# FFN tiles three to eight: the first four column blocks computed by token halves, and one query transpose six slots sooner

## The chip, the core and the metric

The kernel runs on one core of a Trainium2 chip. The core has a matrix engine (TensorE, PE in the profile), three engines that compute on vectors (VectorE or DVE, ScalarE or ACT, GpSimd or POOL), and a sync engine (SyncE or SP) that here only issues DMAs. TensorE reads its operands from the on-chip memory SBUF and writes to the accumulators in PSUM, of which this kernel uses eight banks of 128 x 512 fp32. Every matmul instruction is preceded by a weight load (PEld), which the profile shows on a row of its own. The metric is the device time of one launch in microseconds (us), the median of several runs.

## The reference

Two stages follow each other. The first is linear attention over 8 batches, 8 heads, 576 positions and a head size of 64; the second is a multiplicative feed-forward network (FFN) on its 4608 tokens.

```
r = max(x, 0);  phi(x) = [r * cos(theta), r * sin(theta)]      # 64 -> 128 features, for q and k
kv  = sum over positions of phi(k) v^T         z = sum of phi(k)
x   = (phi(q) kv) / (phi(q) z + 1e-6)          # 4608 tokens x 512
a, b = x @ w1, x @ w2                          # 512 -> 1024 each
out = ((a * b) @ w3) @ w_out                   # 1024 -> 1024 -> 512
```

## The kernel before

**Tiles.** The tokens of all batches are laid in a row and cut into nine FFN tiles of 512 tokens, which the code numbers 0 to 8. A tile's input `xT` has features on the partitions and tokens along the free dimension. Because a batch has 576 tokens, a tile's tokens come from two batches, in pieces of 128 (or 64) that finish at different times.

**How a tile's input is made.** For each piece c of batch b the plan names these steps: `q b c` makes the query features `qp` (DVE the cosine half, ACT the sine half, L494 to L502; a number at the end leaves only that many heads to ACT and the rest to DVE), `qd b c` transposes them by a DMA of SP's queue into `qpT` (L521), `n b c` multiplies them with `kvs` on TensorE (L580), `d b c` divides by the denominator on DVE (L591 to L593) into `xblk`, and `xd b c` transposes that by another DMA of SP's queue into its columns of `xT` (L613). `k`, `v` and `kv` prepare the state `kvs` of a batch; `kv` is 40 matmuls of 65 columns (L548).

**How a tile is computed.** `ffn_groups(t)` is a generator; each `f t` of the plan runs it to its next `yield`, which is a step. For each of eight column blocks of 128 (`jc`) there are two steps. In the first, four matmuls of 512 tokens with `w1b` (L667) give `aT`, and ACT copies it to SBUF as `asb` (L708). In the second, four matmuls with `w2b` give `bT`, and DVE multiplies both into `abT` (L714). The PSUM tiles come from a pool of four banks, `ffn_tile()`, taken in rotation: a step's bank is the one of four PSUM tiles earlier, and it is free when ACT or DVE has read it. Tiles 0 and 1 compute their first four blocks differently, in halves and quarters of the tokens (`on_half`), two blocks to a bank.

For the second stage, `w3 @ w_out` has been multiplied once into `w34b`. Tiles 2 to 7 (`SEVEN`) use seven products of half-sized blocks in place of eight (`seven_products`, L794), for which DVE forms sums of quarters of `abT` (`sums`, L774) and adds the products up (L802). In the pairs of tiles the last products of one tile and the first steps of the next take turns, as the plan has it:

```
f 3; k 5 3 4; k 5 2; v 5 1 V; lg 6 k 0; q 5 3
f 4
f 3; lt 7 k 0; d 4 3
f 4; qd 5 0
f 4; n 4 4
```

**What sets the order.** The order is written by hand in `PLAN`, read from top to bottom; each engine and each queue executes its own instructions in that order, and waits by semaphores. In a line, `f t` comes first and then what its neighbours do. `lt` and `sx` let POOL wait for the DMA transpose that was named last before it in the plan, and then issue a load or a store; `lg` and `sg` do the same with the latest `asb`.

In the code, tile 4 is the one whose first step `f 4` stands in the lines above (L139); `qd 6 1` stands at L189, between `xd 6 4` (L184) and `xd 6 2` (L190), and `n 6 1`, which reads its result, at L193. The features `q 6 1 4` stand at L179.

Of the kernel before, what the change touches and what calls it, by code (L numbers as in the profile page):

```python
# [11 lines left out]
BF16 = mybir.dt.bfloat16  # L12
# [4 lines left out]
P = 128  # L17
# [162 lines left out]
f 5  # L180
f 5; xd 6 0
f 5
f 5; n 6 4
f 5; d 6 4; xd 6 4  # L184
f 5
f 5; n 6 2
f 5
f 6; v 7 3 V; n 6 3
f 6; qd 6 1; d 6 2; q 7 2; sg  # L189
f 6; xd 6 2; gx 0; q 7 4 2  # L190
f 6; d 6 3; sg; q 7 0
f 6; qd 7 4; k 7 4; xd 6 3
# [65 lines left out]
f 8  # L258
f 8"""
SEVEN = (2, 3, 4, 5, 6, 7)  # L260
ON_POOL = (8,)
NKP, NVA, NQP, NRQ, NRV, NT3 = 1, 2, 1, 2, 2, 3

# [50 lines left out]
def kernel(  # L314
# [11 lines left out]
    nc = tc.nc  # L326
# [10 lines left out]
    fsb = ctx.enter_context(tc.tile_pool(name="fsb", bufs=3))  # L337
# [21 lines left out]
    w1b = const.tile([P, 4, DFF], BF16, name="w1b")  # L359
    w2b = const.tile([P, 4, DFF], BF16, name="w2b")  # L360
# [59 lines left out]
    def load_q04():  # L420
# [5 lines left out]
                      in_=q[0, :, 0:512, :].rearrange("h (p j) d -> p h (j d)", j=4))  # L426
# [197 lines left out]
    newest = [None]  # L624
# [29 lines left out]
    def ffn_tile():  # L654

        return ffn_pool[0].tile([P, 512], FP32, name="ffnps")

    def ffn_groups(t):
        x = xT[t]
        abT = None  # L660

        def new_abT():
            return fsb.tile([P, 8, 512], BF16, name="abT", bufs=1)

        def products(out, w, jc, tok):
            for kc in range(4):
                nc.tensor.matmul(out, lhsT=w[:, kc, ts(jc, 128)], rhs=x[:, kc, tok],  # L667
                                 start=(kc == 0), stop=(kc == 3))

        def on_half(half):  # L670

            for pair in range(2):
                a, b = ffn_tile(), ffn_tile()
                if pair == 0:
                    for quarter in range(2):
                        for i in range(2):
                            for ps, w in ((a, w1b), (b, w2b)):
                                products(ps[:, ds(256 * i + 128 * quarter, 128)], w, i,
                                         ds(256 * half + 128 * quarter, 128))
                            if half == 0 and quarter == 0 and i == 0:  # L680
                                yield
                        if quarter == 0:
                            yield
                else:
                    for ps, w in ((a, w1b), (b, w2b)):
                        for i in range(2):
                            products(ps[:, ts(i, 256)], w, 2 + i, ts(half, 256))
                        if half == 0 and w is w1b:
                            yield
                asb = fsb.tile([P, 512], BF16, name="asb")  # L690
                nc.scalar.copy(out=asb[:], in_=a[:, :])
                newest[0] = asb
                nc.vector.tensor_mul(out=abT[:, ts(pair, 2), ts(half, 256)],
                                     in0=asb[:].rearrange("p (i n) -> p i n", i=2),
                                     in1=b[:, :].rearrange("p (i n) -> p i n", i=2))
                yield

        seven = t in SEVEN
        s = [fsb.tile([P, 4, 256], BF16, name=f"s{i}", bufs=1) for i in range(3)] if seven else None
        if t <= 1:  # L700
            abT = new_abT()
            yield from on_half(0)
            yield from on_half(1)
        for jc in range(4 if t <= 1 else 0, 8):
            aT = ffn_tile()
            products(aT[:, :], w1b, jc, slice(0, 512))
            asb = fsb.tile([P, 512], BF16, name="asb")
            nc.scalar.copy(out=asb[:], in_=aT[:, :])  # L708
            newest[0] = asb
            yield  # L710
            bT = ffn_tile()
            products(bT[:, :], w2b, jc, slice(0, 512))
            abT = abT or new_abT()
            nc.vector.tensor_mul(out=abT[:, jc, :], in0=asb[:], in1=bT[:, :])  # L714
            if seven and jc == 3:
                sums(abT, s, 0, 4, 3)
            if seven and jc == 5:
                sums(abT, s, 0, 2, 2, 1)
            if seven and jc == 7:
                sums(abT, s, 2, 2, 2, 1)  # L720
                sums(abT, s, 0, 4, 4)
            yield
# [31 lines left out]
    def A_of(abT, r, c, i0=0, n=4):  # L754

        return abT[:, ds(4 * c + i0, n), ts(r, 256)]
# [10 lines left out]
    def sums(abT, s, i0, n, *which):  # L767

        s3, s2, s4 = (x[:, ds(i0, n)] for x in s)
        a11, a12, a21, a22 = (A_of(abT, r, c, i0, n) for r in range(2) for c in range(2))  # L770
        for i in which:
            out, a, b, op = {3: (s3, a11, a21, ALU.subtract), 1: (a21, a21, a22, ALU.add),
                             2: (s2, a22, s3, ALU.subtract), 4: (s4, a12, s2, ALU.subtract)}[i]
            nc.vector.tensor_tensor(out=out, in0=a, in1=b, op=op)  # L774

    def seven_products(t, abT, s):
# [4 lines left out]
        last = t == NT - 1  # L781
        side = nc.gpsimd if t in ON_POOL else nc.vector
        u3, u4 = (x[:].rearrange("p c m -> p (c m)").bitcast(FP32) for x in (s2, s3))
# [140 lines left out]
    def store_behind_transposes():  # L924

        gate(transposed[0])
        store_next()

    ffn = [ffn_groups(t) for t in range(NT)]
    do = {  # L930
        "f": lambda t: next(ffn[t]), "w": w34_mm, "w3": load_w3, "wo": load_wout, "w12": w12,
# [45 lines left out]
```

## Time and profile before

| | before |
|---|---|
| median of 3 runs | 246.83 us (246.6 to 247.05) |
| the profiled execution's own time | 246.72 us |
| its span in the profile | 244.9 us |
| TensorE busy | 235.6 us, 2035 matmuls |
| VectorE busy | 191.4 us, 455 instructions |
| ScalarE busy | 111.7 us |
| GpSimd busy | 79.8 us |
| granted TensorE clock | 1.00 |

The span is the part of the time that the profile covers; 1.8 us lie around it. A row of the timeline has the start in us, the length in us, the engine, the line of the kernel, the operation, what it writes and reads, the shape, and in brackets how long the engine stood idle before it and what ended that. The ends of matmuls are modelled, so the pace of TensorE is read from one group's start to the next one's. In a row of the windows, the numbers are the length of the stretch and then, for each engine, the busy time and the number of instructions.

### The profile page before, as it was taken

Reading aid. Unit: us, or ns where it says so; the run is one execution under the profiler, and the core shown is the slowest. Engines: PE = TensorE matmul, PEld = TensorE weight load, DVE = VectorE, ACT = ScalarE, POOL = GpSimd, SP = SyncE. Lnnn points to the kernel's source line nnn. Section 1 sums busy time; section 2 is a strip of 40 time slices with the busy share of each in tenths; the row PEclk is TensorE's granted clock in tenths of the full one; section 3 lists DMA queues with packets and bytes.
Section 4 is the critical chain, followed back from the end, with each engine's and each line's share of the span. In section 5 each row is a group of like instructions: output and inputs, shape, how many; then the busy total and the mean of one; then the engine's idle time right before and its main releaser. Section 6 shows DMA issues by size and latency. Waiting matters only on the chain.

```text
span 244.9 us, 5395 instructions
## 1 busy us (share of the span) xinstructions
PE 235.6 (96%) x2035; PEld 144.5 (59%) x2035; DVE 191.4 (78%) x455; ACT 111.7 (46%) x198; POOL 79.8 (33%) x152
## 2 busy tenths in 40 slices
PE   8899999999999999999996999999989999999994
PEld 2589544566964544765583548555835675484443
DVE  6876577968888758999889798999999688776320
ACT  2833333677655733835472435737164412322321
POOL 8754887634503124107206103401020031084000
PEclk9999999999999999999999999999999999999999
DMA  7999999999999899969997998699297627499963
GB/s 198 191 196 199 197 179 193 199 198 174 154 166 162 131 153 169 197 115 148 141 176 99 192 174 110 72 175 155 33 232 136 119 44 181 88 272 315 262 185 128
DMA packets 84938, 40.47 MB, mean 165 GB/s; under 512 B 48048, under 2 KB 82096, under 8 KB 84912
## 3 DMA queue, kind: packets, MB, share of 16 engines
q0 software_dynamic: 37616, 23.60, 66.4%
q1 hardware_dynamic: 47296, 16.52, 39.3%
q8 instruction: 16, 0.26, 0.4%
q14 instruction: 10, 0.08, 0.1%
HBM read 38.80 MB, written 9.44 MB: 197 GB/s over the span
## 4 chain that ended last, share of the span: by engine, by line
PE 81%; DVE 10%; DMA 6%; issue 1%; DVEq 0%; ACT 0%; ACTq 0%
PE ffnps L667 47%; PE ffnps L794 7%; PE ffnps L729 7%; PE unread L456 4%; PE ffnps L473 4%; DMA xT<-xblk 3%; PE pnum L548 3%; PE pnum L580 3%; DMA qpT<-qp 2%; PE ffnmore L794 1%; DVE xblk L593 1%; DVE kp L494 1%; PE pst L566 1%; DVE qp L494 1%; PE pst L620 1%
## 5 line engine op out<-in xcount | busy, mean ns | idle before, releaser
L667 PE MATMUL ffnps<-xT,w1b 128*128 128x512 bf16 (+2 forms) x352 | 76.0, 340 | 2.4 <-DMA xT<-xblk 2.2
L667 PE MATMUL ffnps<-xT,w2b 128*128 128x512 bf16 (+2 forms) x352 | 76.0, 340 | 0.0
L708 ACT CAST asb<-ffnps 128x512 bf16<-128x512 f32 x64 | 37.5, 585 | 79.0 <-PE ffnps L667 60.5
L714 DVE TENSOR_TENSOR abT<-asb,ffnps 128x512 bf16<-128x512 bf16 x64 | 43.5, 682 | 20.8 <-PE ffnps L667 20.6
L667 PEld LDWEIGHTS <-w1b 128*128 128x128 bf16 x352 | 31.6, 98 | 30.0 <-issue 3.0
L667 PEld LDWEIGHTS <-w2b 128*128 128x128 bf16 x352 | 31.4, 98 | 26.8
L593 DVE TENSOR_TENSOR xblk<-pnum,den 128x512 bf16<-128x512 f32 (+1 forms) x39 | 26.9, 691 | 1.3
L498 ACT ACTIVATE kp<-kf,sinv 128x512 bf16<-128x512 bf16 (+4 forms) x33 | 20.4, 654 | 2.6 <-DMA kf<-in_k_dram 2.6
L418 POOL COPY seen<-xT 128x1 bf16<-128x1 bf16 x6 | 1.1, 189 | 61.1 <-DMA xT<-xblk 61.1
L729 PE MATMUL ffnps<-w34b,abT 128*128 128x512 bf16 x88 | 20.8, 379 | 0.0
L794 PEld LDWEIGHTS <-abT 128*128 128x128 bf16 x192 | 18.5, 98 | 3.2
L580 PEld LDWEIGHTS <-qpT 128*128 128x128 bf16 x320 | 15.1, 98 | 7.3 <-DMA qpT<-qp 1.6
L498 ACT ACTIVATE qp<-qs,sinv 128x512 bf16<-128x512 bf16 (+6 forms) x30 | 18.3, 626 | 1.7 <-DMA qpT<-qp 0.7
L580 PE MATMUL pnum<-kvs,qpT 128*128 128x65 bf16 x312 | 16.1, 194 | 1.1 <-DMA qpT<-qp 1.1
L794 PEld LDWEIGHTS <-s 128*128 128x128 bf16 x144 | 14.0, 98 | 2.0
L494 DVE TENSOR_SCALAR kp<-kf,cosv 128x512 bf16<-128x512 bf16 (+1 forms) x40 | 14.6, 385 | 0.0
L473 PE MATMUL ffnps<-early,w3T 128*128 128x512 bf16 x64 | 14.3, 379 | 0.0
L418 POOL COPY seen<-asb 128x1 bf16<-128x1 bf16 x13 | 2.8, 218 | 34.5 <-ACT asb L708 34.5
L729 PEld LDWEIGHTS <-abT 128*128 128x128 bf16 x88 | 8.1, 98 | 8.5
L794 PE MATMUL ffnps<-w34b,abT 128*128 128x256 bf16 x96 | 12.4, 273 | 0.0
L494 DVE TENSOR_SCALAR qp<-qs,cosv 128x512 bf16<-128x512 bf16 (+1 forms) x35 | 11.9, 349 | 0.5 <-issue 0.5
L513 POOL COPY va<-vs 128x512 bf16<-128x512 bf16 (+1 forms) x13 | 8.4, 654 | 10.9 <-DMA vs<-in_v_dram 10.3
(127 smaller groups left out, 322.0 us busy)
## 6 DMA issues: line engine op xcount, KB each, us to landing
out_dram<-osb SPq DMA_DIRECT2D x9, 256.0 KB, 3.5
kf<-in_k_dram POOLq DMA_DIRECT2D x7, 320.0 KB, 6.9
early<-in_moe_w_dram POOLq DMA_DIRECT2D x16, 128.0 KB, 5.1
qs<-in_q_dram POOLq DMA_DIRECT2D x6, 320.0 KB, 8.0
vs<-in_v_dram POOLq DMA_DIRECT2D x6, 320.0 KB, 8.1
kf<-in_k_dram POOLq DMA_DIRECT2D x7, 256.0 KB, 7.2
qs<-in_q_dram POOLq DMA_DIRECT2D x6, 256.0 KB, 9.5
vs<-in_v_dram POOLq DMA_DIRECT2D x6, 256.0 KB, 9.3
```

The lines of the kernel that those rows point to most:

```text
L456: nc.tensor.matmul(unread[:, :], lhsT=zeros[:, 0:128], rhs=zeros[:], start=True, stop=True)
L473: nc.tensor.matmul(acc[:, :], lhsT=w3T[:, lc, :], rhs=woutb[:, lc, :], start=(lc == 0), stop=(lc == 7))
L494: nc.vector.tensor_scalar(out=dst[:R, c, :, 0:D], in0=rows[:R], scalar1=0.0, scalar2=cosv[:R, at:at + 1], op0=ALU.max, op1=ALU.mult)
L498: nc.scalar.activation(out=dst[:R, c, 0:n, D:F], in_=rows[:R, 0:n], func=ACTF.Relu, scale=sinv[:R, at:at + 1], bias=0.0)
L513: (copy or nc.gpsimd.tensor_copy)(out=att_of(b)["va"][:R, c, :, 0:D], in_=raw[b, "v"][:R, :, c, :])
L580: nc.tensor.matmul(nt[:, h // 4, ds((h % 4) * 65, 65)], lhsT=qpT[:, h, ds(at, 128)], rhs=kvs[:, h, :], start=True, stop=True)
L593: nc.vector.tensor_tensor(out=xblk[rows, g0:g0 + ng], in0=n4[:, :, :, 0:D], in1=den[rows, 0:ng].unsqueeze(3).to_broadcast([R, ng, 4, D]), ...
L667: nc.tensor.matmul(out, lhsT=w[:, kc, ts(jc, 128)], rhs=x[:, kc, tok], start=(kc == 0), stop=(kc == 3))
L708: nc.scalar.copy(out=asb[:], in_=aT[:, :])
L714: nc.vector.tensor_mul(out=abT[:, jc, :], in0=asb[:], in1=bT[:, :])
L729: nc.tensor.matmul(ops[:, :], lhsT=abT[:, jc, ts(ms, 128)], rhs=w34b[:, jc, :], start=(jc == 0), stop=(jc == 7))
L794: nc.tensor.matmul(into[:, ts(ms, 256)], lhsT=a[:, kc, ts(ms, 128)], rhs=b[:, kc, :], start=(ms == 0 and kc == 0), stop=(ms == 1 and kc == 3))
```

## The change

Two things change. In tiles 2 to 7 the first four column blocks are no longer computed one block at a time over 512 tokens, but two blocks at a time over 256 tokens: first both pairs of blocks for one half of the tokens, then both for the other half. Tile 3 takes the upper half first, the other tiles the lower half. A step still fills one PSUM bank, with eight matmuls of 256 columns in place of four of 512; the number of steps, of ACT copies and of DVE multiplications stays, and the DVE operation for the differences of quarters (`sums(..., 3)`) follows the eighth step as before. The matmuls with the tile's first half wait only for the transposes that write that half.

Secondly the DMA transpose `qd 6 1` moves up by six lines of the plan, ahead of `xd 6 4` in SP's queue. In the list of instructions, SP's queue has just these two exchanged; GpSimd's is the same as before.

```diff
 f 5
-f 5; n 6 4
+f 5; n 6 4; qd 6 1
 f 5; d 6 4; xd 6 4
...
 f 6; v 7 3 V; n 6 3
-f 6; qd 6 1; d 6 2; q 7 2; sg
+f 6; d 6 2; q 7 2; sg
...
 SEVEN = (2, 3, 4, 5, 6, 7)
+BY_HALF = {t: (1, 0) if t == 3 else (0, 1) for t in range(2, 8)}
...
-        for jc in range(4 if t <= 1 else 0, 8):
+        if t in BY_HALF:
+            for half, pair in [(h, p) for h in BY_HALF[t] for p in range(2)]:
+                aT = ffn_tile()
+                for i in range(2):
+                    products(aT[:, ts(i, 256)], w1b, 2 * pair + i, ts(half, 256))
+                asb = fsb.tile([P, 512], BF16, name="asb")
+                nc.scalar.copy(out=asb[:], in_=aT[:, :])
+                newest[0] = asb
+                yield
+                bT = ffn_tile()
+                for i in range(2):
+                    products(bT[:, ts(i, 256)], w2b, 2 * pair + i, ts(half, 256))
+                abT = abT or new_abT()
+                nc.vector.tensor_mul(out=abT[:, ts(pair, 2), ts(half, 256)],
+                                     in0=asb[:].rearrange("p (i n) -> p i n", i=2),
+                                     in1=bT[:, :].rearrange("p (i n) -> p i n", i=2))
+                if seven and half == BY_HALF[t][1] and pair == 1:
+                    sums(abT, s, 0, 4, 3)
+                yield
+        for jc in range(4 if t <= 1 or t in BY_HALF else 0, 8):
             aT = ffn_tile()
             products(aT[:, :], w1b, jc, slice(0, 512))
```

## The prediction

> **What bounds the kernel.** I read the page's busy shares first, then TensorE's waits, then its timeline for the place of each, then the same stretches for VectorE and SP.
>
> ```profile
> PE 235.6 (96%) x2035; PEld 144.5 (59%) x2035; DVE 191.4 (78%) x455; ACT 111.7 (46%) x198; POOL 79.8 (33%) x152
> ```
>
> ```profile
> PE ffnps L667 <- DMA xT<-xblk: 2.2, 1, 2.2
> ...
> PE pnum L580 <- DMA qpT<-qp: 1.1, 1, 1.1
> ```
>
> TensorE is busy nearly throughout, and two of its three longest waits are for DMA transposes. They are these:
>
> ```profile
> 127.54 1.04 PE L794 MATMUL ffnps<-early,abT 128*128 128x256 bf16 x8
> 130.72 1.02 PE L667 MATMUL ffnps<-xT,w1b 128*128 128x512 bf16 x4 [2.15 <-DMA xT<-xblk]
> ...
> 136.17 1.03 PE L667 MATMUL ffnps<-xT,w2b 128*128 128x512 bf16 x4
> ```
>
> ```profile
> 181.03 1.03 PE L667 MATMUL ffnps<-xT,w2b 128*128 128x512 bf16 x4
> 183.18 0.43 PE L580 MATMUL pnum<-kvs,qpT 128*128 128x65 bf16 x8 [1.11 <-DMA qpT<-qp]
> ...
> 187.76 1.03 PE L667 MATMUL ffnps<-xT,w2b 128*128 128x512 bf16 x4
> ```
>
> A group takes 0.87 us from start to start (pace below), so the first gap is 130.72 - 127.54 - 0.87 = 2.31 us, before tile 4's first step; the second is 183.18 - 181.03 - 0.86 = 1.29 us, before `n 6 1`. Both have their late transposes in SP's queue:
>
> ```profile
> 113.87 1.33 SPq L613 DMA_TRANSPOSE xT<-xblk  x1
> 119.44 1.19 SPq L613 DMA_TRANSPOSE xT<-xblk  x1
> 122.22 2.27 SPq L613 DMA_TRANSPOSE xT<-xblk  x1
> ...
> 173.00 1.19 SPq L613 DMA_TRANSPOSE xT<-xblk  x1
> 176.34 1.17 SPq L613 DMA_TRANSPOSE xT<-xblk  x1
> 177.60 2.17 SPq L521 DMA_TRANSPOSE qpT<-qp  x1
> ```
>
> Counted off against the plan, these are `xd 3 3`, `xd 4 0`, `xd 4 1`, then `xd 6 0`, `xd 6 4`, `qd 6 1`. Tile 4's lower half is `xd 3 2` and `xd 3 3`, issued by 113.87; what it waits for is `xd 4 1` in its upper half, issued at 122.22 and landed at 130.7.
>
> But VectorE is the second bound. Busy time by stretch (length, then PE, PEld, DVE, ACT, POOL, then granted clock, DMA and GB/s):
>
> ```profile
> 153.00:159.40 6.40, 6.40 (x42) 3.34 (x40) 6.33 (x19) 4.48 (x9) 2.75 (x5) 1.00 0.71 75
> ...
> 172.00:178.00 6.00, 6.00 (x68) 4.88 (x67) 5.59 (x14) 0.80 (x2) 0.00 (x0) 1.00 0.18 33
> 178.00:183.20 5.20, 4.08 (x20) 1.69 (x19) 5.06 (x15) 3.47 (x7) 1.49 (x4) 1.00 0.96 230
> 183.20:190.00 6.80, 6.80 (x73) 3.97 (x74) 6.66 (x18) 2.68 (x5) 0.00 (x0) 1.00 0.74 152
> 190.00:196.00 6.00, 6.00 (x48) 3.87 (x45) 3.58 (x9) 2.58 (x5) 0.00 (x0) 1.00 0.60 115
> ```
>
> In 153 to 159.4 VectorE works 6.33 of 6.40 us, in 178 to 190 11.72 of 12.0 us. It does not become free when TensorE's wait goes, so a gain has to pass through it. From 190 on it has room (3.58 of 6.0).
>
> **Part 1, halves: what goes at tile 4.** The lower half landed long before 128.4, so step one can start at 128.41. The upper half is first read in step five, over four us later, when `xd 4 1` has landed (130.7). The 2.31 us wait goes. What is late next is VectorE, through the four PSUM banks.
>
> ```profile
> 130.59 0.69 DVE L802 TENSOR_TENSOR osb<-ffnps,s 128x512 f32<-128x512 f32 x1
> 132.66 0.69 DVE L802 TENSOR_TENSOR osb<-ffnps,s 128x512 f32<-128x512 f32 x1 [0.19 <-PE ffnps L794]
> 134.91 1.36 DVE L714 TENSOR_TENSOR abT<-asb,ffnps 128x512 bf16<-128x512 bf16 x2
> ...
> 137.30 0.69 DVE L714 TENSOR_TENSOR abT<-asb,ffnps 128x512 bf16<-128x512 bf16 x1 [0.77 <-PE ffnps L667]
> ```
>
> From 128 to 132.66 VectorE has other work and idles only 0.19 us, so it can run 0.19 us sooner, no more. I walk through the banks. Step a0 starts at 128.41, tile 3's last product at 129.28, b0 at 130.15. a1 needs the bank that the row at 130.59 reads, free at 131.28. `n 4 4` and b1 follow until 133.3, a2 until 134.1. b2 needs the bank of b0, which VectorE reads in the first of the two at 134.91, now 134.72, free at 135.40. So b2 starts at 135.40 where it started at 136.17: 0.77 us of the 2.31 come through, and 1.54 turn into a wait for a bank.
>
> Further on the gain meets a load.
>
> ```profile
> 147.40 0.19 POOL L418 COPY seen<-xT 128x1 bf16<-128x1 bf16 x1 [11.73 <-DMA xT<-xblk]
> 147.85 0.68 POOL L375 DMA_DIRECT2D kf<-in_k_dram  x1 [0.27 <-issue]
> ...
> 153.26 0.40 ACT L498 ACTIVATE kp<-kf,sinv 128x128 bf16<-128x128 bf16 x1 [2.13 <-DMA kf<-in_k_dram]
> 153.26 0.35 DVE L494 TENSOR_SCALAR kp<-kf,cosv 128x512 bf16<-128x512 bf16 x1
> ```
>
> ACT waits 2.13 us for keys that are loaded behind an SP transpose, and VectorE takes the same keys at the same 153.26, with no idle time before it only because it was busy until then. If the load moves with the rest, 0.77 us survive. If SP's chain, whose members hang on rows that move by 0.19 us only, sets the load, VectorE waits and about 0.2 us survive. I take the middle, 0.45 us; nothing in the trace decides it.
>
> **Part 1, halves: what it costs.** 32 matmuls of 512 become 64 of 256 in each of six tiles: 192 matmuls and 192 weight loads more. The pace of both forms is in the trace, the short one in tile 0:
>
> ```profile
> 24.09 1.04 PE L667 MATMUL ffnps<-xT,w1b 128*128 128x256 bf16 x8
> 24.96 1.04 PE L667 MATMUL ffnps<-xT,w2b 128*128 128x256 bf16 x8
> 25.84 1.03 PE L667 MATMUL ffnps<-xT,w1b 128*128 128x512 bf16 x4
> ...
> 220.68 1.03 PE L667 MATMUL ffnps<-xT,w1b 128*128 128x512 bf16 x4
> 221.54 1.03 PE L667 MATMUL ffnps<-xT,w2b 128*128 128x512 bf16 x4
> ...
> 233.63 1.03 PE L667 MATMUL ffnps<-xT,w2b 128*128 128x512 bf16 x4
> ```
>
> Eight of 256 take 0.87 to 0.88 us; four of 512 take (233.63 - 220.68) / 15 = 0.863. The added weight loads are hidden in that pace. A step so costs 0.007 to 0.017 us more, 0.01 say; 48 steps, 0.48 us. In tiles 4, 5 and 6 (24 steps) VectorE or a bank is waited for anyway, so half of it shows: 0.24 us, between 0 and 0.8. VectorE's multiplication with a split output is priced in tiles 0 and 1, 686 ns (L693) against 682 ns (L714):
>
> ```profile
> L714 DVE TENSOR_TENSOR abT<-asb,ffnps 128x512 bf16<-128x512 bf16 x64 | 43.5, 682 | 20.8 <-PE ffnps L667 20.6
> ...
> L693 DVE TENSOR_TENSOR abT<-asb,ffnps 128x512 bf16<-128x512 bf16 x8 | 5.5, 686 | 3.4 <-ACT asb L691 2.1 <-PE ffnps L667 1.3
> ```
>
> For 24 of them this is 0.1 us at most, taken as nothing. At the start of tiles 2, 3, 5, 6 and 7 the waits list has no wait for `xT`, so the halves remove nothing there; they only keep a wait from arising if these tiles start sooner. In tile 3 the order of the halves only changes which transposes come first.
>
> A rule of the Trainium skill speaks against this part. The page "TensorE: Matmul & The Clock Gate", section "Back-to-back issue gap", says that a stream of weight loads and matmuls runs at some 81 ns for 128 columns and 131 ns for 512. On a straight line a 256-column matmul would take an estimated 98 ns, two of them 65 ns more than one of 512, and 192 such pairs would add some 12 us. The same section's other formula, for a single gap, gives 218 against 216 ns and adds 0.5 us. The rows above (0.863 / 4 = 216 ns, 0.87 / 8 = 109 ns) agree with the second and not with the first.
>
> **Part 2, `qd 6 1` sooner.** Nothing is added. SP issues it after `xd 6 0` (173.00 + 1.19 = 174.2) when its features are there:
>
> ```profile
> 173.15 0.28 DVE L501 TENSOR_SCALAR qp<-qs,sinv 128x256 bf16<-128x256 bf16 x1
> ...
> 186.19 0.68 DVE L714 TENSOR_TENSOR abT<-asb,ffnps 128x512 bf16<-128x512 bf16 x1
> ```
>
> VectorE finishes the features at 173.43, ACT's share is earlier, so it issues at 174.2 in place of 177.60. With the same 5.6 us to landing (177.60 to 183.18) it lands at 179.8; TensorE wants it at 181.9. Margin 2.1 us, and DMA is quiet then (0.18 and 33 GB/s in the stretch from 172 to 178). `xd 6 4`, now behind it, waits for an `xblk` and starts at 176.34; `qd 6 1` is issued by 175.4, or 176.4 at 2.17 us of issue, so it slips by 0.1 us at most, and tile 7 reads it over 20 us later. On POOL's queue no `lt` or `sx` stands between the two places, so no gate changes.
>
> The 1.29 us go, and a bank is late next. From `n 6 1` at 181.89, b5 comes after it and five more groups: 181.89 + 0.26 + 5 x 0.863 = 186.5. It needs the bank that VectorE reads at 186.19, free at 186.87. Before, b5 started at 187.76: 0.89 us come through. This holds shifted, if all runs sooner by part 1. After 190 VectorE has 2.4 us of idle time per 6 and catches up; to the end no row of TensorE waits for a DMA.
>
> **Sum.** -0.45 - 0.89 + 0.24 = -1.1 us on the profiled execution's 246.72 us, which is 0.11 below the median of 246.83: 245.6 us.
>
> **Rivals.**
> - All of it comes through: VectorE and the load follow at once. -2.31 - 1.29 + 0.24: 243.4 us. For it: VectorE's idle pieces between 132 and 151 follow TensorE, as at 137.30. Against: the 134.91 row's bank.
> - VectorE takes all back: part 1 leaves 0 to 0.2 us because of the load, and part 2's lead is lost before 190. With the dearer steps, 246.5 us. For it: 11.72 of 12.0 us busy. Against: the room after 190.
> - The change doesn't do what it says in part 2: the sooner transpose takes longer among other transfers and lands after 181.9, over 2.1 us worse than now. Then only part 1 counts: 246.5 us.
> - Slower: the added 192 weight loads don't hide in these tiles, where ACT, DVE and transposes run beside them, as they do in tile 0. Each is 98 ns in its row (below), so 18.8 us if all show, 265 us; from some 9 ns each (1.1 + 0.49 us over 192) on the kernel is slower than before by 0.2%; a fifth visible gives 249.4 us. Against: also the 256-column products (L794) keep 0.87 us.
>
> ```profile
> L667 PEld LDWEIGHTS <-w1b 128*128 128x128 bf16 x352 | 31.6, 98 | 30.0 <-issue 3.0
> ```
>
> **How the numbers follow.** 0.2% of 246.83 is 0.49 us, about what a measurement of this kernel can tell from no change. The forecast has 0.50 (own range 244.9 to 246.2), all through 0.13, VectorE takes all back 0.18, transpose still late 0.06, slower by weight loads 0.06, and 0.07 for what I don't see, mostly transfers that fall together differently, half of it slower. Faster: 0.47 of the first, 0.13, and 0.09 of the rest, 0.69; slower 0.06 + 0.04 and 0.02 of the taken-back case, 0.12; same 0.19. The range 243.5 to 247.1 leaves out the weight loads, about half of the all-through case and some of the unseen, under 2 in 10.
>
> **What would show it.** Right: tile 4's first group, now 256 columns, right after the product at 127.5 with no wait for `xT`; a TensorE wait of over 1 us for VectorE some seven groups later; `n 6 1` without a wait; a short wait for VectorE before 187; VectorE's row at 153 waiting up to half a us for `kf`. Groups of eight 256-column matmuls start 0.87 us apart. Wrong: a pace over 0.9 us, `qpT` still a wait of TensorE, or new waits for `xT` or `kf` over 1 us.

## The result and the profile after

| | before | after |
|---|---|---|
| median of 5 runs | 246.60 us (246.38 to 247.05) | 245.57 us (245.15 to 249.01) |
| the profiled execution's own time | 246.72 us | 245.66 us |
| its span | 244.9 us | 243.9 us |

The ratio of the times is 0.995, with an interval from 0.9933 to 0.9967: the change saves 1.0 us, and the two profiled executions differ by 1.06 us. Runs more than 1.5% above the fastest one of the same kernel, such as that of 249.01 us, count as slow, and this ratio is taken without them. In two later measurements, below, the gain was seen again in one and not in the other.

The busy shares of the page after differ in one thing, 192 more matmuls and weight loads:

```profile
PE 235.1 (96%) x2227; PEld 162.4 (67%) x2227; DVE 190.0 (78%) x455; ACT 111.8 (46%) x198; POOL 80.9 (33%) x152
```

TensorE's waits after hold neither of the two transposes any more. In place of them stand two others (us in total, times, longest):

```profile
PE ffnps L668 <- ACT asb L711: 1.0, 1, 1.0
...
PE ffnps L668 <- DVE abT L718: 0.3, 1, 0.3
```

TensorE's timeline after, from tile 4's start to the last group of the second stage:

```profile
127.93 1.04 PE L814 MATMUL ffnps<-early,abT 128*128 128x256 bf16 x8
128.81 1.04 PE L668 MATMUL ffnps<-xT,w1b 128*128 128x256 bf16 x8
...
131.43 1.04 PE L668 MATMUL ffnps<-xT,w1b 128*128 128x256 bf16 x8
...
134.45 1.04 PE L668 MATMUL ffnps<-xT,w2b 128*128 128x256 bf16 x8
135.81 1.03 PE L668 MATMUL ffnps<-xT,w1b 128*128 128x256 bf16 x8 [0.33 <-DVE abT L718]
136.68 1.44 PE L549 MATMUL pnum<-va,kp 128*128 128x65 bf16 x40
...
153.49 0.42 PE L581 MATMUL pnum<-kvs,qpT 128*128 128x65 bf16 x8
153.75 1.04 PE L668 MATMUL ffnps<-xT,w2b 128*128 128x256 bf16 x8
155.77 1.03 PE L668 MATMUL ffnps<-xT,w1b 128*128 128x256 bf16 x8 [0.98 <-ACT asb L711]
...
162.88 1.43 PE L549 MATMUL pnum<-va,kp 128*128 128x65 bf16 x40
...
181.10 1.04 PE L668 MATMUL ffnps<-xT,w2b 128*128 128x256 bf16 x8
181.97 0.42 PE L581 MATMUL pnum<-kvs,qpT 128*128 128x65 bf16 x8
...
186.62 1.03 PE L668 MATMUL ffnps<-xT,w2b 128*128 128x512 bf16 x4
187.49 1.44 PE L549 MATMUL pnum<-va,kp 128*128 128x65 bf16 x40
...
238.61 1.91 PE L766 MATMUL ffnps<-w34b,abT 128*128 128x256 bf16 x16
```

The same groups before, as far as the prediction doesn't show them:

```profile
137.90 1.44 PE L548 MATMUL pnum<-va,kp 128*128 128x65 bf16 x40
...
154.69 0.42 PE L580 MATMUL pnum<-kvs,qpT 128*128 128x65 bf16 x8
...
162.86 1.44 PE L548 MATMUL pnum<-va,kp 128*128 128x65 bf16 x40
...
188.62 1.44 PE L548 MATMUL pnum<-va,kp 128*128 128x65 bf16 x40
...
239.67 1.91 PE L746 MATMUL ffnps<-w34b,abT 128*128 128x256 bf16 x16
```

Laid side by side these rows say where the time went. The groups of 40 matmuls are the `kv` steps, which I count by batch from 1.

| TensorE starts (us) | before | after | after - before |
|---|---|---|---|
| fourth `kv` | 114.83 | 115.22 | +0.39 |
| tile 4, first step | 130.72 | 128.81 | -1.91 |
| fifth `kv` | 137.90 | 136.68 | -1.22 |
| `n 5 1` | 154.69 | 153.49 | -1.20 |
| sixth `kv` | 162.86 | 162.88 | +0.02 |
| `n 6 1` | 183.18 | 181.97 | -1.21 |
| seventh `kv` | 188.62 | 187.49 | -1.13 |
| last group | 239.67 | 238.61 | -1.06 |

The execution after was 0.39 us behind when the stretch began, for a reason that stays open. Then tile 4's wait went and gave a lead of 1.2 us, which was lost again within 10 us after `n 5 1`. The wait before `n 6 1` went, and what it gave lasted to the end. So the whole gain of this pair of executions is the second part's. The lead was lost to the keys of batch 6. VectorE's rows after the change, at the banks that the prediction argued from and at these keys, and then ACT's row at the keys:

```profile
131.05 0.69 DVE L822 TENSOR_TENSOR osb<-ffnps,s 128x512 f32<-128x512 f32 x1
...
132.84 0.68 DVE L822 TENSOR_TENSOR osb<-ffnps,s 128x512 f32<-128x512 f32 x1
...
135.08 1.27 DVE L718 TENSOR_TENSOR abT<-asb,ffnps 128x512 bf16<-128x512 bf16 x2
...
153.33 0.39 DVE L495 TENSOR_SCALAR kp<-kf,cosv 128x512 bf16<-128x512 bf16 x1 [1.14 <-DMA kf<-in_k_dram]
...
186.20 0.68 DVE L718 TENSOR_TENSOR abT<-asb,ffnps 128x512 bf16<-128x512 bf16 x1
```

```profile
153.33 0.40 ACT L499 ACTIVATE kp<-kf,sinv 128x128 bf16<-128x128 bf16 x1 [3.41 <-DMA kf<-in_k_dram]
```

The keys came at 153.33, before the change at 153.26. VectorE now stood still for 1.14 us for them and ACT for 3.41, and TensorE for 0.98 at 155.77 for the copy that ACT made behind them.

Why the keys did not move with the rest stands in GpSimd's queue, which issues the loads. After the change:

```profile
127.61 0.19 POOL L419 COPY seen<-xT 128x1 bf16<-128x1 bf16 x1 [9.21 <-DMA xT<-xblk]
...
136.13 0.19 POOL L419 COPY seen<-xT 128x1 bf16<-128x1 bf16 x1 [6.46 <-DMA xT<-xblk]
136.72 0.88 POOL L386 DMA_DIRECT2D kf<-in_k_dram  x1 [0.41 <-DVE qp L495]
...
148.94 0.19 POOL L419 COPY seen<-xT 128x1 bf16<-128x1 bf16 x1 [9.47 <-DMA xT<-xblk]
149.39 0.68 POOL L376 DMA_DIRECT2D kf<-in_k_dram  x1 [0.27 <-ACT va L514]
```

and before it:

```profile
130.71 0.19 POOL L418 COPY seen<-xT 128x1 bf16<-128x1 bf16 x1 [12.70 <-DMA xT<-xblk]
...
132.74 0.20 POOL L418 COPY seen<-xT 128x1 bf16<-128x1 bf16 x1
132.85 0.88 POOL L385 DMA_DIRECT2D kf<-in_k_dram  x1
```

The copies into `seen` are the gates `lt`: GpSimd goes on when a transpose has landed. The gate on `xd 4 1` opened 3.1 us sooner, and the loads behind it went out sooner. The next gate, on `xd 4 2`, opened at 136.13 instead of by 132.74, and the loads behind that one at 136.72 instead of 132.85. The gate ahead of batch 6's keys, on `xd 5 0`, opened at 148.94, where it was 147.40. That the sooner loads delay the transposes fits the order of these rows, but no run here measures it by itself.

### The profile page after: what moved, and what is told of

Same layout as the page of the kernel before. It is cut to its first block, busy times and chain, and to the rows that moved or that the text cites. A ratio compares the mean times of both kernels' runs of the same rounds, so it can differ in the third digit from the quotient of the medians.

```text
span 243.9 us, 5778 instructions
## 1 busy us (share of the span) xinstructions
PE 235.1 (96%) x2227; PEld 162.4 (67%) x2227; DVE 190.0 (78%) x455; ACT 111.8 (46%) x198; POOL 80.9 (33%) x152
## 4 chain that ended last, share of the span: by engine, by line
PE 71%; DMA 15%; DVE 6%; POOL 5%; issue 2%; ACT 1%; DVEq 0%; POOLq 0%; ACTq 0%
PE ffnps L668 43%; PE ffnps L814 11%; PE ffnps L749 7%; DMA kf<-in_k_dram 4%; DMA w2b<-in_moe_w_dram 4%; PE pnum L549 3%; PE pnum L581 3%; DMA q<-in_q_dram 2%; DMA early<-in_moe_w_dram 2%; DMA xT<-xblk 2%; PE ffnmore L814 1%; POOL w2b L922 1%; POOL early L407 1%; POOL early L413 1%; DVE w3T L464 1%
## 5 line engine op out<-in xcount | busy, mean ns | idle before, releaser
L668 PE MATMUL ffnps<-xT,w1b 128*128 128x256 bf16 (+2 forms) x448 | 76.2, 303 | 1.3 <-ACT asb L711 1.0
L668 PE MATMUL ffnps<-xT,w2b 128*128 128x256 bf16 (+2 forms) x448 | 76.2, 303 | 0.0
L668 PEld LDWEIGHTS <-w1b 128*128 128x128 bf16 x448 | 41.1, 98 | 20.4 <-issue 2.0
L668 PEld LDWEIGHTS <-w2b 128*128 128x128 bf16 x448 | 40.8, 98 | 19.6 <-issue 0.2
L495 DVE TENSOR_SCALAR kp<-kf,cosv 128x512 bf16<-128x512 bf16 (+1 forms) x40 | 13.3, 353 | 1.1 <-DMA kf<-in_k_dram 1.1
```

What stands on the lines that cost most here:

```text
L495: nc.vector.tensor_scalar(out=dst[:R, c, :, 0:D], in0=rows[:R], scalar1=0.0, scalar2=cosv[:R, at:at + 1], op0=ALU.max, op1=ALU.mult)
```

## The experiments

**The question.** Theory A: the lead of part 1 is lost because the keys of batch 6 land on a chain of loads and transposes of its own, and part 2's gain is real where that transpose is late. Theory B is what stands against it and differs from run to run: the prediction's sum in the first runs, later that the sooner keys help only together with the change, or that VectorE takes the gain back through the PSUM banks. Every kernel ran with the kernel before on its chip. The times on these chips, called A, B and C, spread much more than in the first measurement, up to 8.9 us for one kernel, so I give the difference of the medians of all runs, with a 95% interval from drawing the runs anew, and beside it the ratio of the times, taken as in the result above.

| kernel | runs | median (range), us | minus before on the same chip, us | ratio to before |
|---|---|---|---|---|
| *chip A:* before | 35 | 247.74 (243.74 to 252.59) | | |
| transpose sooner only | 12 | 246.31 (245.52 to 248.80) | -1.44 [-2.34, 0.45] | 1.003 [0.999, 1.008] |
| halves only | 12 | 247.55 (246.14 to 249.38) | -0.19 [-1.65, 0.90] | 1.005 [1.000, 1.010] |
| the change, keys' gate earlier | 12 | 245.81 (244.50 to 248.69) | -1.94 [-3.03, -0.28] | 0.999 [0.994, 1.004] |
| transpose, halves in tile 4 alone | 12 | 246.42 (245.04 to 248.05) | -1.32 [-2.28, -0.42] | 1.000 [0.996, 1.004] |
| *chip B:* before | 35 | 247.32 (244.93 to 253.64) | | |
| before again | 12 | 246.36 (244.67 to 250.18) | -0.96 [-2.11, -0.09] | 0.998 [0.994, 1.002] |
| the change again | 12 | 247.35 (245.59 to 250.75) | +0.03 [-1.17, 1.39] | 1.003 [0.999, 1.007] |
| the change, keys by `asb` | 12 | 244.78 (244.02 to 248.38) | -2.54 [-3.65, -1.44] | 0.992 [0.988, 0.996] |
| transpose, keys by `asb` | 12 | 245.02 (243.70 to 250.54) | -2.30 [-3.69, -1.37] | 0.991 [0.987, 0.995] |
| *chip C:* before | 25 | 247.52 (246.12 to 249.31) | | |
| keys by `asb` only | 12 | 245.53 (244.48 to 248.57) | -1.99 [-2.75, -0.95] | 0.990 [0.987, 0.993] |
| halves, keys by `asb` | 12 | 245.96 (244.70 to 248.40) | -1.56 [-2.29, -0.03] | 0.994 [0.990, 0.997] |
| transpose, keys by `asb` | 6 | 244.44 (244.12 to 245.26) | -3.09 [-3.64, -2.32] | 0.985 [0.982, 0.989] |
| the change a third time | 8 | 245.70 (244.58 to 249.22) | -1.82 [-2.51, 1.03] | 0.991 [0.987, 0.995] |

"Before again" says how far a difference of medians can be trusted: the same kernel differs from itself by 0.96 us, with an interval that leaves out zero, while its ratio is 1 within the interval. So I call a gain shown where both columns say so, which holds for the five rows with the keys by `asb` and for no other row; for the rest the profiles carry the readings, one execution each. Four stretches of TensorE's timeline, from start to start, and VectorE's wait for the keys:

| profiled execution | fourth `kv` to tile 4 | VectorE waits for the keys | fifth to sixth `kv` | `n 6 3` to `n 6 1` | sixth `kv` to the last group |
|---|---|---|---|---|---|
| before | 15.89 | 0 | 24.96 | 5.86 | 76.81 |
| after | 13.59 | 1.14 | 26.20 | 4.62 | 75.73 |
| transpose only | 14.24 | 2.56 | 27.69 | 4.57 | 75.52 |
| halves only | 13.58 | 3.91 | 29.22 | 4.99 | 76.05 |
| change, gate earlier | 13.59 | 1.03 | 26.44 | 4.62 | 75.73 |
| transpose, tile 4 | 13.59 | 0.97 | 25.99 | 4.57 | 76.52 |
| before again | 13.59 | 0.73 | 25.75 | 4.58 | 75.52 |
| change again | 13.59 | 3.08 | 29.21 | 4.63 | 75.73 |
| change, keys by `asb` | 13.58 | 0 | 24.91 | 4.63 | 75.73 |
| transpose, keys by `asb`, chip B | 13.59 | 0 | 24.82 | 4.57 | 76.52 |
| keys by `asb` only | 13.59 | 0 | 24.81 | 5.82 | 76.78 |
| halves, keys by `asb` | 13.59 | 0 | 25.91 | 5.83 | 76.89 |
| transpose, keys by `asb`, chip C | 13.59 | 0 | 25.12 | 4.57 | 75.52 |
| change, third time | 13.59 | 0.66 | 25.88 | 4.62 | 75.71 |

**Each part alone.** First the transpose without the halves:

```diff
-f 5; n 6 4
+f 5; n 6 4; qd 6 1
...
-f 6; qd 6 1; d 6 2; q 7 2; sg
+f 6; d 6 2; q 7 2; sg
```

> The kernel before with the query transpose six slots sooner and no halves. Theory A (all of the gain is the sooner transpose, the halves' gain at tile 4 is lost again in the wait for keys at 153 us): about 1.1 us faster than before, the same as the changed kernel within 0.3 us; TensorE's wait before n 6 1 gone. Theory B (the prediction: both parts give, 0.45 less 0.24 and 0.89 us): 0.9 us faster than before and slower than the changed kernel by 0.2 us. Rival C (the halves are needed for it): no gain.

Then the halves with the plan of before:

```diff
+BY_HALF = {t: (1, 0) if t == 3 else (0, 1) for t in range(2, 8)}
...
+        if t in BY_HALF:
...
-        for jc in range(4 if t <= 1 else 0, 8):
+        for jc in range(4 if t <= 1 or t in BY_HALF else 0, 8):
```

> The halves alone, the query transpose at its old place. Theory A: the same as before within 0.3 us (0 to 0.2 us slower by the dearer steps); TensorE waits about 1.3 us before n 6 1, VectorE waits about 1 us for the keys at 153 us, and TensorE stands at the same place at 160 us as in the kernel before. Theory B: 0.2 us faster. A rival in which the halves' gain comes through: 0.8 us or more faster.

The transpose alone was 1.44 us faster on the median, the halves alone 0.19, neither clear of zero, and by the ratio neither gains anything. The profiles say more, though not what was expected for the halves: TensorE stood still before `n 6 1` for 0.4 us in place of 1.3, VectorE waited 3.91 us for the keys in place of 1, and TensorE fell behind the kernel before. VectorE at the keys, and the sixth `kv` on TensorE, with the halves alone:

```profile
155.50 0.35 DVE L495 TENSOR_SCALAR kp<-kf,cosv 128x512 bf16<-128x512 bf16 x1 [3.91 <-DMA kf<-in_k_dram]
```

```profile
165.39 1.43 PE L549 MATMUL pnum<-va,kp 128*128 128x65 bf16 x40
```

TensorE led the kernel before by 1.7 us at the fifth `kv` (136.17 against 137.90) and was 2.5 us behind it at the sixth: the keys came 2.2 us later than before the change. Wherever VectorE waits for the keys, the sixth `kv` follows 9.5 to 10.7 us after it takes them, whatever tile 4 did. Where VectorE does not wait, the distance is 9.5 to 10.6 us too, so it does not prove by itself that the keys set the time; the edits to the keys' gate below test that. Theory A stands so far, and part 1 can end on either side of zero.

**Fewer halves, and a gate at another place.** The transpose with the halves in tile 4 alone, the one tile that waited:

```diff
-BY_HALF = {t: (1, 0) if t == 3 else (0, 1) for t in range(2, 8)}
+BY_HALF = {4: (0, 1)}
```

> The sooner transpose, and halves in tile 4 alone. The dearer steps of the five other tiles go (40 steps of 0.01 us, of which the prediction has some 0.2 us show). Theory A and B: 0 to 0.3 us faster than the changed kernel. Rival E (the halves of another tile save a wait too): slower than the changed kernel by 0.3 us or more.

Its median is 1.32 us under that of before, its ratio 1.000. The change itself did not run on chip A; the nearest there is the next kernel, which also has another gate. Against that one it is 0.62 [-0.93, 1.57] us behind, so the halves of the other tiles can't be told from nothing. No profile with halves in all six tiles has a wait for a tile's input. Without them in tile 3 it waits 1.54 us in the profile of the keys alone, below, and in the profile of this kernel tiles 3 and 6 wait 0.48 and 0.85 us:

```profile
108.72 1.02 PE L668 MATMUL ffnps<-xT,w1b 128*128 128x512 bf16 x3 [0.48 <-DMA xT<-xblk]
...
178.51 1.02 PE L668 MATMUL ffnps<-xT,w1b 128*128 128x512 bf16 x3 [0.85 <-DMA xT<-xblk]
```

The whole change with the load of batch 6's keys five lines up, still behind a gate on a transpose:

```diff
-f 4
+f 4; lt 6 k 1
...
-f 4; lt 6 k 1; xd 5 4
+f 4; xd 5 4
```

> The changed kernel with the load of the second half of batch 6's keys gated on an earlier transpose, five lines of the plan sooner. Theory A: VectorE's wait of 1.1 us for the keys goes, TensorE's wait of about 1 us before 156 us goes, and the time falls by 0.7 to 1.1 us against the changed kernel, to about 244.6 us. Rival D (VectorE is full from 153 to 190 us, or the sooner load delays the transposes beside it): 0.3 us or less, new waits for xT or qpT.

The gate opened at 147.60, only 1.3 us sooner than after the change, and VectorE still waited 1.03 us. The wait was expected to go and did not. The edit hardly moved the cause, so the run tells nothing about Theory A.

**Both kernels again.** No edit: the kernel before and the change, with a second profile of each.

> The kernel before once more, for its spread and a second profile. Both theories: no difference. If tile 4's wait for xT is a fixed property of the kernel, it is 2.3 us again and the last transpose of tile 4 lands 8.4 us after its issue; if it comes from transfers that fall together differently from one execution to the next, it differs by more than 1 us.

> The changed kernel once more, beside the others on the same chip. Theory A (only the sooner transpose gains; the time that the halves save at tile 4 is lost in the wait for keys near 153 us): 1.0 to 1.3 us faster than before, VectorE waits 1 us or more for the keys, and the last kv of the stretch (batch 6) starts 9.5 to 9.9 us after they land. Theory B (the prediction): 1.1 us faster with VectorE's wait at half a us.

This was the surprise. In the second profile of the kernel before, tile 4 and `n 6 1` start without any wait, on TensorE:

```profile
128.54 1.03 PE L667 MATMUL ffnps<-xT,w1b 128*128 128x512 bf16 x3
...
181.15 0.42 PE L580 MATMUL pnum<-kvs,qpT 128*128 128x65 bf16 x8
```

Neither wait that the change removes is fixed in the kernel. Of the six profiles without halves in tile 4, one has its wait in full (2.3 us), one a part of it (0.65), four none; of the five without the sooner transpose, three have the wait before `n 6 1` (1.2 to 1.3 us), one has 0.4, one none. So in these profiles tile 4's wait is rare and that before `n 6 1` frequent. The change's second profile lost 4.3 us between the fifth and sixth `kv` (29.21 against 24.91 where the keys don't wait), and its median on chip B is that of before, where both theories had it about 1 us faster.

**The keys by another gate.** Here the load of batch 6's keys hangs no longer on a transpose but on the newest copy `asb`, six lines earlier. In the change:

```diff
-f 4; n 5 0; v 6 0 G
+f 4; lg 6 k 1; n 5 0; v 6 0 G
...
-f 4; lt 6 k 1; xd 5 4
+f 4; xd 5 4
```

> The changed kernel with the load of the second half of batch 6's keys gated on an ACT copy of tile 4 in place of a transpose, issued near 141 us in place of 149. Theory A: the keys land before 151 us, VectorE's wait for them is gone, and the time falls by 0.7 to 1.1 us against the changed kernel. Rival D (VectorE is full from there to 190 us, or the transposes beside the load land later): 0.3 us or less, and a new wait for qpT or xT on TensorE.

The same edit with the transpose sooner, without the halves:

> The sooner query transpose and the sooner load of keys, without halves. If the halves' gain at tile 4 is real and only hidden by the keys, this is slower than the same with halves by 0.5 us or more, with TensorE waiting for xT before tile 4 or another tile. If the halves give nothing, the two are the same within 0.3 us.

Both are 2.3 to 2.5 us faster than before, and the change with this edit is 2.58 [1.31, 3.93] us faster than without it, more than the 0.7 to 1.1 expected. GpSimd issues the load 8 us sooner than in the change, and VectorE finds the keys there:

```profile
141.40 0.68 POOL L376 DMA_DIRECT2D kf<-in_k_dram  x1 [0.27 <-issue]
```

```profile
152.36 0.35 DVE L495 TENSOR_SCALAR kp<-kf,cosv 128x512 bf16<-128x512 bf16 x1
```

Theory A is borne out where it can be changed: with the keys there, fifth to sixth `kv` takes 24.8 to 24.9 us in these two, and nothing is lost on the way. Between the two no difference by the halves can be told (0.25 [-1.04, 1.16] us); but the one without them had no wait at tile 4 in its profile, so it does not show a lead of the halves kept.

**The parts again, with the keys sooner.** On chip C: the keys alone, the keys with the halves, the keys with the transpose, and the change itself. The edits are those above.

> The kernel before, with only the load of batch 6's keys moved up to a gate that opens with tile 4's copies; neither part of the change. Theory A (the landing of the keys sets TensorE from tile 4 on): VectorE takes the keys without a wait, near 152.4 us when TensorE's fifth kv starts near 137; the sixth kv starts 24.9 us after the fifth (24.8 to 25.0 in the two kernels that had this load sooner); the time is 1.3 to 2.5 us under the kernel before. Theory B (the sooner load only helps where the halves or the sooner transpose make the lead): 0 to 0.5 us under the kernel before.

> The keys sooner and the halves, without the sooner transpose. Theory A: against the keys alone the halves cost the dearer steps, 0.2 us in the stretch from the third to the fourth kv and 0.2 us from the sixth kv to the end, and gain what wait for tile 4's input remains in the kernel without them (0 to 2.3 us, by execution); on the median -1.0 to +0.4 us against the keys alone. Theory B (VectorE's banks take the gain back): +0.4 us, and the wait of tile 4 reappears as a wait for a bank of over 1 us.

> The keys sooner and the query transpose sooner, without the halves, a second time on another chip. Theory A: 2.0 to 3.0 us under the kernel before as the first time (2.3), and under the keys alone by the wait ahead of the multiplication that reads the transpose, 0 to 1.3 us. Theory B (that transpose is late only in some executions, so its move is worth little on the median): within 0.3 us of the keys alone.

> The changed kernel once more, on a third chip beside the kernel before. Theory A (the time before the keys is lost at the keys, the sooner transpose comes through where it was late): 0 to 1.2 us under the kernel before, with VectorE waiting 1 to 3 us for batch 6's keys, and the sixth kv 9.5 to 10.7 us after VectorE takes them. Theory B (the first measurement's gain belongs to one chip): within 0.5 us of the kernel before on the median.

The keys alone give 1.99 us, without either part of the change: Theory A. The interval of 24.81 us and VectorE's start without a wait, 15.3 us after the fifth `kv`, are as expected. How much of the 1.99 us is the wait for the keys is not shown: the two profiles of the kernel before exceed the 24.81 us by only 0.15 and 0.94 us. With the keys sooner this stretch is not always as short, either: with the halves it took 25.91 us, where TensorE waited for another query transpose (0.61 us at 151.53), and with the transpose 25.12. The transpose gives 1.09 [0.33, 2.00] us on top, and the profiles show the wait that goes. `n 6 1` on TensorE with the keys alone (an execution of 248.57 us, one of its longest), with the keys and the halves (246.70 us), and then with the keys and the transpose:

```profile
185.04 0.43 PE L580 MATMUL pnum<-kvs,qpT 128*128 128x65 bf16 x8 [1.08 <-DMA qpT<-qp]
```

```profile
183.03 0.43 PE L581 MATMUL pnum<-kvs,qpT 128*128 128x65 bf16 x8 [1.04 <-DMA qpT<-qp]
```

```profile
181.15 0.42 PE L580 MATMUL pnum<-kvs,qpT 128*128 128x65 bf16 x8
```

The two together came out 3.09 us under the kernel before, just past the 2.0 to 3.0 expected. No gain of the halves shows: +0.43 us [-0.53, 2.00] against the keys alone, at the upper end of what Theory A allowed and as much as its rival said; but the rival's wait for a bank of over 1 us does not appear. The change itself came out 1.82 us faster on the median, with an interval that includes zero, and with a ratio of 0.991 [0.987, 0.995]; VectorE waited 0.66 us for the keys, less than the 1 to 3 expected, and the gain was larger than the 0 to 1.2. The best kernel here is the sooner transpose with the sooner keys and no halves: 244.44 us against 247.52 us before and 245.70 us for the change, 1.26 [0.62, 4.02] us better than the latter.

## Why the prediction was right, and where its steps failed

The time, 245.6 us, and the sum, -1.1 us, were met by 245.57 and -1.06. Its three terms were not: the errors cancel, and that they do is luck, as is that the execution profiled before had both waits in full.

- **Tile 4's wait goes: right.** The first group starts 0.88 us behind the product at 127.93, with no wait, and the step's place was right; it read one execution's wait as the kernel's, though, and in four of the six profiles without halves there is none to remove.
- **"b2 needs the bank of b0": wrong.** b2 starts at 134.45, before VectorE reads b0 at 135.08, and the group after it waits 0.33 us for that multiplication. a1 starts at 131.43 in the same way, while VectorE reads the bank that it should need (131.05, 0.69 us long). So banks are not taken in strict rotation here, contrary to the description of the kernel. Judged by these waits, b2 got a bank that had come free earlier, and a3 that of b0. So from the fourth to the fifth `kv` 1.6 us came through, not 0.77, of which 1.2 are left as a lead over the kernel before; and the announced wait of over 1 us for VectorE was 0.33 us. That wait is no price of the halves: four profiles without them, in which tile 4 starts without a wait, have it too (0.34 us).
- **"I take the middle, 0.45 us": wrong, and the lower of the two cases was right.** The load of the keys hung on a chain of its own, as the second case said; of part 1 nothing remained at the sixth `kv` (+0.02 us). The prediction's own sign for this, a wait of over 1 us for `kf`, is what the profile shows (1.14 us). Its reason was only half the cause: the chain did not merely stay, its gate opened 1.5 us later, which the edits to the keys' gate show to matter.
- **The dearer steps, 0.24 us in all: too low, in the share that shows.** The sixth `kv` to the last group holds tiles 6 and 7. Without other waits it takes 75.52 us in three executions without halves, and 75.71 to 75.73 in five with them: 0.2 us in 16 steps, 0.013 us each, within the 0.007 to 0.017 of the prediction. But all of it shows, in tile 6 too, where half was assumed hidden. For tiles 2 to 5 the profiles don't separate it from other changes.
- **The rule on back-to-back pairs.** The Trainium skill's page "TensorE: Matmul & The Clock Gate", section "Back-to-back issue gap", gives about 81 ns for 128 columns and 131 ns for 512. By it a step of eight matmuls of 256 would cost an estimated 0.26 us more than one of four of 512. The 0.013 us a step above, and the groups 0.87 us apart after the change (181.10 to 181.97), hold against it: the added loads hide. Its formula for a single gap, 218 ns for two of 256 against 216 ns for one of 512, gives an estimated 0.010 us a step and agrees.
- **`n 6 1` without a wait: right. That b5 "needs the bank that VectorE reads at 186.19": wrong** in the same way. b5 starts at 186.62, while that multiplication (186.20, 0.68 us long) is running. So the wait's worth came through almost whole, 1.2 us up to `n 6 1` and 1.15 up to the seventh `kv`, where 0.89 was put down. That the gain of the second part lasts to the end was right: after the seventh `kv` only 0.07 us is lost, about what the dearer steps of tile 7 cost.

So the sum was right with 0, 1.2 and 0.15 to 0.2 in place of 0.45, 0.89 and 0.24. Two figures of the rivals do not follow from their own terms: with 0 to 0.2 us of part 1 left, none of part 2 and 0.24 for the steps, "VectorE takes all back" ends at 246.8 to 247.0 us and not at 246.5; and 1.1 + 0.49 us over 192 loads is 8.3 ns each and not 9. Of the rivals, "VectorE takes all back" named the load that took part 1; its second half failed. The weight loads and the late transpose did not come about.

What stays open: whether the change is faster on the average of many chips. It was in the first measurement (0.995 [0.9933, 0.9967]); on chip B it was not (1.003 [0.9988, 1.0071]), and on chip C it was by the ratio (0.991 [0.987, 0.995]), while the interval of the medians includes zero. What made the keys' gate open later after the change was not isolated. Whether the halves protect the other tiles from late inputs, as the waits of tiles 3 and 6 where these have no halves suggest, was not tried with enough profiles to say.

## What to carry to other kernels

A wait on a DMA in one profile is one execution's wait: profile the kernel before a second time before pricing its removal. When a lead is predicted, look for the next transfer that the lead runs into, and at the gate that issues it; here moving that one load gave more on the median (2.0 us) than either part of the change, though part of that gain is unexplained. A pool of PSUM banks should be read from its waits and not assumed to rotate.

## What the runs showed of the hardware that was not expected

The same transpose takes very different times. SP issued `xd 4 1` at 122.22 before and at 122.61 after:

```profile
122.61 1.19 SPq L614 DMA_TRANSPOSE xT<-xblk  x1
```

GpSimd saw it landed at 130.71 and at 127.61, 8.5 and 5.0 us later. In the second profile of the kernel before it took 5.6 us (122.35 to 127.95), so tile 4 had nothing to wait for. The whole kernel's time scatters too: the kernel before ran from 243.74 to 252.59 us on one chip, while its five runs of the first measurement lay within 0.7 us. Moving the transpose and the keys does not take the scatter away for certain: six runs of that kernel lay within 244.12 to 245.26 us on chip C, twelve on chip B within 243.70 to 250.54.
